# A fused attention and FFN kernel: the first FFN pieces cut into quarters that follow the pairs of heads, and a new table of due times

## The chip, the cores and the metric

The kernel runs on one core of one Trainium2 chip. The metric is the time of one execution on the device, in microseconds (us). Before the change the median of 8 runs is 224.05 us, from 223.49 to 226.14.

## What is computed

Two stages follow each other. The first is an attention in which the blocks of K and V are mixed by a matrix that five rounds of row and column normalisation make from `sort_net`. The second is an FFN with a squared ReLU on the attention's output. Cut to what matters, with B = 4 batches, H = 8 heads, S = 768 positions, D = 64, 8 blocks of 96 positions, 3072 tokens, a model width of 512 and a hidden width of 2048:

```python
P = sort_net
for _ in range(5):
    P = exp(P - max(P, -1)); P = P / sum(P, -1); P = P / sum(P, -2)
k_sorted = einsum('bhij,bhjcd->bhicd', P, k_blocks)     # and v_sorted
scores = scale * q_blocks @ k_sorted_blocks.T           # inside each block
attn   = softmax(scores) @ v_sorted_blocks
x   = attn.transpose(0, 2, 1, 3).reshape(3072, 512)
h   = maximum(x @ w_in, 0)
out = (h * h) @ w_out
```

## The kernel before

**The order.** The order of all engines is fixed when the program is built. Each step is an `Op` with an engine, an estimated cost, the steps that it depends on and, for attention steps on TensorE, a due time. `Plan.run` (L117) lays the steps out in time: TensorE takes either the head of the attention list `att` or the head of the FFN list `ffn`. An attention step goes ahead when it can begin earlier, or when its due time has come. Due times (`DUES`, L21) count FFN pieces begun (`chunks`, L150). Each list keeps its own order; the attention list is sorted by due time (L1063). The instructions are then emitted in the order of begin that the plan found, so the plan's costs (`TAIL`, L97, and the extra lateness in `SLACK`, L100) decide what stands behind what on every engine, SyncE's queue of transfers among them. None of the plan's numbers is an instruction; only the order comes out of them.

**The pairs.** Heads are worked on in four pairs per batch. A pair's 128 rows of `xT` are one of the four groups of 128 (kc) over which the FFN's first product sums. The stages of a pair are K and V (sorting by multiplication, L560, copied out of PSUM by L229 on ScalarE or L231 on VectorE), S (scores, L631, then exp on ScalarE, L654 or L663), T (transpose of V, L679), A (attention times V, L814, then a reciprocal and a product on VectorE, L824 and L825) and X (transpose into `xT`: L862 on TensorE, or a DMA transpose on SyncE, L847). In `FIRST` (L53), which orders the first half of the first batch, a capital letter gives the copy to ScalarE and a small one to VectorE.

**The batches.** The first batch is handled in two halves of 384 positions each. From the second on, K and V come in another layout. V is multiplied (V, `s_nat`, L714), copied to `vn`, written to device memory (`v_way`, L738) and read back in blocks (`vblk`, L744). K is multiplied (N, `s_nat` too), copied to `kn` and turned by a DMA transpose (Z, `kx`, L766), and q likewise (`qT`, L789). All of these transfers and the stores of results (L937) go out through SyncE, one after the other.

**The FFN.** `ffn_unit` (L880) works on half a batch, 384 tokens: 16 pieces `up`, each of four multiplications hp (L893, one per kc) into one PSUM tile of the pool `psf`, each followed by a ReLU (L901, ScalarE) and a square (L904, VectorE); then three tiles of 128 tokens, each with four pieces `down` of four multiplications op (L921). Every piece `up` depends on the `xT` of all four pairs (L883, L908). `psf` has three buffers; the first batch's K and V and the q transposes use them too, ahead of the FFN. Attention steps share two further PSUM tiles, `p2`, in turn.

**The loads.** GpSimd issues the loads of q, k, v and the weights. w_in and w_out come in four quarters each (L325 and L358). Until the FFN begins, the program fills longer waits of TensorE with multiplications by a matrix of ones (`fill`, L389); the emitting loop (L1070) decides where.

Of the kernel before, what the change touches and what calls it, by code (L numbers as in the profile page):

```python
# [8 lines left out]
FP32 = mybir.dt.float32  # L9
# [9 lines left out]


DUES = {  # L21
    (0, "K"): (-15.0, -1.0, 10, 10),
    (0, "S"): (-1.0, 11.0, 11.0, 15.0),
    (0, "T"): (-1.5, 10.0, 13.5, 19.5),
    (0, "A"): (14.0, 14.5, 18.0, 21.5),
    (0, "X"): (16.0, 23.0, 24.5, 25.0),
    (0, "W"): (1.5,),
    (1, "V"): (4.0, 20.5),
    (1, "Q"): (31.0,),
    (1, "N"): (None, 33.0),  # L30
    (1, "Z"): (None, None, 43.0, 44.0),
    (1, "S"): (33.5, 41.0, 43.0, 48.0),
    (1, "A"): (39.5, 41.5, 45.5, 52.0),
    (1, "X"): (48.0, 49.5, 49.5, 55.0),
    (2, "L"): (52.0,),
    (2, "N"): (64.0, 69.5),
    (2, "V"): (74.5, 91.5),
    (2, "Z"): (84.0, 86.0, 95.5, 96.5),
    (2, "S"): (88.5, 93.0, 97.5, 100.5),
    (2, "A"): (95.0, 99.5, 102.0, 104.0),  # L40
    (2, "X"): (96.5, 105.5, 107.5, 109.5),
    (3, "L"): (110.5,),
    (3, "N"): (120.0, 126.0),
    (3, "V"): (123.0, 141.5),
    (3, "Z"): (130.5, 138.0, 153.0, 155.5),
    (3, "S"): (143.5, 153.0, 157.5, 159.5),
    (3, "A"): (149.5, 155.0, 160.5, 162.5),
    (3, "X"): (158.5, 160.0, 161.5, 166.5),
}

FIRST = ("K0 V0 K1 v1 S0 t0 S1 k2 t1 A0 V2 S2 K3 t2 A1 V3 X0 A2 S3 t3 x1 A3 X2 x3")  # L53


class Op:


    def __init__(self, eng, cost, fn, deps, due=0, mode="full"):
        self.mode = mode  # L60
        self.engs = (eng,) if isinstance(eng, str) else eng
        self.cost = (cost,) if not isinstance(cost, tuple) else cost
        self.fn, self.deps, self.due = fn, [d for d in deps if d is not None], due
        self.begin = self.end = None


class Ring:
# [24 lines left out]
class Plan:  # L92
# [1 line left out]

    TAIL = {"PE": 0.0, "ACT": 0.09, "DVE": 0.06, "POOL": 0.0, "DMA": 0.0, "SP": 0.0, "WAY": 0.6}  # L97
    HOP = 0.06
    SWITCH = 0.1
    SLACK = {"DMA": 2.5, "WAY": 1.0}  # L100

    def __init__(self):
        self.att, self.ffn, self.rest = [], [], []
# [13 lines left out]
    def run(self):  # L117
        free = {e: 0.0 for e in self.TAIL}
        att, ffn, rest = list(self.att), list(self.ffn), list(self.rest)
        done, chunks, mode = [], 0, "full"  # L120
        self.gaps = []
        while att or ffn or rest:
            best = None
            for op in rest:
                r = self.ready(op)
                if r is None:
                    continue
                s, c, e = min(((max(r, free[e]), c, e) for e, c in zip(op.engs, op.cost)),
                              key=lambda x: x[0] + x[1])
                if best is None or s < best[0][0]:  # L130
                    best = ((s, s + c), op, e, c)
            heads = []
            for q in (att, ffn):
                if q:
                    r = self.ready(q[0])
                    if r is not None:
                        heads.append((max(r, free["PE"]), q))
                        continue
                heads.append((None, q))
            (sa, _), (sf, _) = heads  # L140
            pick = None
            if sa is not None and (sf is None or sa < sf - 0.02
                                   or (att[0].due <= chunks and sa <= sf + 0.1)):
                pick = (sa, att)
            elif sf is not None:
                pick = (sf, ffn)
            if pick and (best is None or pick[0] <= best[0][0]):
                s, q = pick
                op = q.pop(0)
                chunks += q is ffn  # L150
                e, c = "PE", op.cost[0] + self.SWITCH * (op.mode != mode)
                mode = op.mode
                op.gap = s - free["PE"]
                if s - free["PE"] > 0.01:
                    self.gaps.append((op, s - free["PE"]))
            else:
                (s, _), op, e, c = best
                rest.remove(op)
            op.begin, op.end, op.eng = s, s + c, e
            free[e] = s + c - self.TAIL[e]  # L160
            done.append(op)
        return sorted(done, key=lambda o: o.begin)
# [3 lines left out]
def kernel(  # L166
# [12 lines left out]
    B, H, S, D = q.shape  # L179
# [11 lines left out]
    KC = d_model // 128  # L191
# [6 lines left out]
    ffn = ctx.enter_context(tc.tile_pool(name="ffn", bufs=2))  # L198
    ps1 = ctx.enter_context(tc.tile_pool(name="ps1", bufs=1, space=bass.MemoryType.PSUM))
    ps2 = ctx.enter_context(tc.tile_pool(name="ps2", bufs=1, space=bass.MemoryType.PSUM))  # L200
    psf = ctx.enter_context(tc.tile_pool(name="psf", bufs=3, space=bass.MemoryType.PSUM))
# [9 lines left out]
    plan = Plan()  # L211
    rvn, rvb = Ring(2), Ring(3)
    r1, r2, rf, rh1, rh2, rob = Ring(1), Ring(2), Ring(3), Ring(3), Ring(2), Ring(3)
# [81 lines left out]
    landed = {}  # L295
# [200 lines left out]
    x_done = {}  # L496
# [201 lines left out]
    def s_nat(b, g, t, due):  # L698

        if t == 2:  # L700
            m, oldm = rvn.take()
        evs = []
        for hp in (2 * g, 2 * g + 1):
            slot, old = r2.take()
            if t == 1:
                m, oldm = rkn.take()

            def mm(e, hp=hp, slot=slot):
                src = qkv[b][t].rearrange("p (g h) x -> p g (h x)", h=HP)
                w = w_t[:, HP // 2 * b + g, :, :].rearrange("p c i -> p (c i)")  # L710
                for h in range(2):
                    r = slice(32 * (2 * (hp % 2) + h), 32 * (2 * (hp % 2) + h + 1))
                    for c in range(4):
                        nc.tensor.matmul(  # L714
                            out=p2[slot][32 * c:32 * (c + 1), h, 0:NA * D],
                            lhsT=w[r, :],
                            rhs=src[r, g, NA * D * c:NA * D * (c + 1)],
                            start=True, stop=True, tile_position=(r.start, 32 * c))

            def ev(e, hp=hp, slot=slot, m=m):  # L720
                dst = (vn_r[m][:, :, 2 * (hp % 2):2 * (hp % 2) + 2, 0:D] if t == 2
                       else kn_r[m])
                copy(e, dst, p2[slot][:, :, 0:NA * D].rearrange("p e (a d) -> p a e d", d=D))

            pe = plan.add("PE", 0.15, mm, [landed[b, t, HP * g, 0], built["t"]] + old, due,
                          mode="tile")
            readers[b].append(pe)
            op = plan.add(AD, cost_f(2 * NA * D), ev, [pe] + oldm)
            r2.use(slot, pe, op)
            evs.append(op)  # L730
            if t == 1:
                rkn.use(m, op)
                k_nat[b, hp] = m, op
        if t == 1:
            return

        def write(e):
            nc.sync.dma_start(out=v_way[b, g].rearrange("a p x -> p a x"),  # L738
                              in_=vn_r[m].rearrange("p a h x -> p a (h x)"))

        w, oldw = rvb.take()

        def read(e):
            nc.sync.dma_start(  # L744
                out=vb_r[w].rearrange("p i h x -> p (i h x)"),
                in_=v_way[b, g].rearrange("a (c i) x -> (a c) (i x)", i=NB))

        wr = plan.add("SP", 0.33, write, evs + ([loaded(b)] if b > 1 else []))
        slow = 6.0 if b == 1 else 2.0
        there = plan.add("WAY", slow, lambda e: None, [wr])  # L750
        rd = plan.add("SP", 0.33, read, [there] + oldw)
        back = plan.add("WAY", slow, lambda e: None, [rd])
        rvn.use(m, *evs, there)
        rvb.use(w, back)
        v_blk[b, g] = w, back
# [124 lines left out]
    def ffn_unit(g):  # L880
        t0 = HS * g
        b, hf = g // 2, g % 2
        xs = [x_done[b, hp, hf] for hp in range(HP)]  # L883
        t = {}
        n2, old2 = rh2.take()
        sq = []
        for nt in range(NT):
            def up(e, nt=nt):
                if nt == 0:
                    t["h2"] = ffn.tile([128, NT, HS], BF16, tag="h2", name="h2")  # L890
                t["hp", nt] = psf.tile([128, 512], FP32, tag="pf", name="hp")
                for kc in range(KC):
                    nc.tensor.matmul(  # L893
                        out=t["hp", nt][:, 0:HS],
                        lhsT=w_in_bf[:, kc, 128 * nt:128 * (nt + 1)],
                        rhs=xT[:, kc, t0:t0 + HS],
                        start=(kc == 0), stop=(kc == KC - 1))
# [6 lines left out]
                nc.vector.tensor_tensor(  # L904
                    out=t["h2"][:, nt, :], in0=t["h1", nt], in1=t["h1", nt], op=ALU.mult)

            sf, old = rf.take()
            pe = plan.add("PE", 0.65, up, xs + [landed["w_in", nt // 4]] + old, ffn=True)  # L908
            s1, old1 = rh1.take()
            r = plan.add("ACT", cost_f(HS)[0], relu, [pe] + old1)  # L910
            s = plan.add("DVE", 0.355, square, [r] + old2)
# [196 lines left out]
```

The softmax here doesn't subtract the row's maximum and nothing guards it: scores larger than these inputs give would overflow.

## Time and profile before

| What | us |
|---|---|
| median of 8 runs | 224.05 |
| the profiled execution's own time | 223.92 |
| its span | 222.1 |
| TensorE busy (fillers among it) | 213.3 |
| ScalarE busy | 120.8 |
| VectorE busy | 102.8 |
| first FFN multiplication begins | 22.19 |
| last multiplications begin (L955, 32 of them) | 214.69 |

The span runs from the first to the last event of the profile; 1.8 us of the execution's own time lie outside it. A busy time counts how long an engine had an instruction in work; neighbouring multiplications overlap, so the distance from one start to the next tells the price of one better than its length does. In a timeline each line gives start, length, engine, line, operation, output and input, and the number of neighbouring instructions that are drawn together.

The chain of waits that ended last consists of TensorE for 76% and of DMA for 16% of the span, most of the latter the loads of w_in and w_out up to 40.86 us.

### The profile page before, as it was taken

What the parts mean: (1) busy time and instruction counts of PE and PEld (TensorE: products, weight loads), DVE (VectorE), ACT (ScalarE), POOL (GpSimd) and SP (SyncE); (2) the same over time, 40 slices, a digit from 0 to 9 for tenths busy, and PEclk for the clock granted to TensorE, in tenths of its full rate; (3) what the DMA queues carried; (4) which work ended last, traced back from release to release, by engine and by line L of the source; (5) the groups of instructions that cost most, each with busy time, mean ns of one, the idle gap of its engine ahead of it and who ended that gap; (6) DMA issues with size and microseconds to landing.
All of it is one profiled execution on the core that took longest, in us unless ns stands there. A gap on an engine that the chain in (4) does not pass through costs nothing.

```text
span 222.1 us, 5101 instructions
## 1 busy us (share of the span) xinstructions
PE 213.3 (96%) x2049; PEld 119.9 (54%) x2065; DVE 102.8 (46%) x291; ACT 120.8 (54%) x249; POOL 26.5 (12%) x49
## 2 busy tenths in 40 slices
PE   8998999999999999999999999999799999999993
PEld 2576665446665555445665465446455455456562
DVE  6778476444773347502676056405655155015300
ACT  4665887217875178517863278229473276147421
POOL 7973230000000600000000330000000000000000
PEclk9999999999999999999999999999999999999999
DMA  5999999998633599189943599558982510120012
GB/s 70 200 203 207 209 206 215 209 260 231 157 75 86 96 221 221 20 227 220 199 112 84 127 182 214 119 148 188 207 173 82 118 49 3 47 94 0 3 62 80
DMA packets 46583, 31.22 MB, mean 141 GB/s; under 512 B 26016, under 2 KB 41632, under 8 KB 46560
## 3 DMA queue, kind: packets, MB, share of 16 engines
q0 software_dynamic: 12736, 13.63, 37.3%
q1 hardware_dynamic: 33824, 17.27, 31.0%
q8 instruction: 16, 0.26, 0.5%
q14 instruction: 7, 0.06, 0.1%
HBM read 29.70 MB, written 8.72 MB: 173 GB/s over the span
## 4 chain that ended last, share of the span: by engine, by line
PE 76%; DMA 16%; POOL 3%; ACT 1%; issue 1%; DVE 1%; SPq 0%; ACTq 0%
PE op L921 34%; PE hp L893 31%; DMA w_out_bf<-in_moe_w_out_dram 10%; DMA w_in_bf<-in_moe_w_in_dram 4%; PE p L631 3%; PE p L814 3%; DMA vblk<-v_way 2%; PE op L955 2%; PE p L714 2%; POOL vb L300 1%; POOL kb L300 1%; DMA p_sb<-in_sort_net_dram 1%; ACT h L901 1%; DVE h L904 0%; PE qtp L511 0%
## 5 line engine op out<-in xcount | busy, mean ns | idle before, releaser
L893 PE MATMUL hp<-xT,w_in_bf 128*128 128x384 bf16 x512 | 88.9, 326 | 0.0
L921 PE MATMUL op<-w_out_bf,h 128*128 128x512 bf16 x352 | 83.2, 379 | 1.2 <-DMA w_out_bf<-in_moe_w_out_dram 0.3
L904 DVE TENSOR_TENSOR h<-h 128x384 bf16<-128x384 bf16 x128 | 44.5, 355 | 62.8 <-ACT h L901 62.3
L901 ACT ACTIVATE h<-hp 128x384 bf16<-128x384 f32 x128 | 61.7, 495 | 19.3 <-PE hp L893 15.8
L893 PEld LDWEIGHTS <-w_in_bf 128*128 128x128 bf16 x512 | 48.1, 98 | 32.1 <-issue 1.0
L921 PEld LDWEIGHTS <-h 128*128 128x128 bf16 x368 | 34.1, 98 | 37.9 <-issue 1.3
L229 ACT COPY ob<-op 128x512 f32<-128x512 f32 (+1 forms) x24 | 13.6, 568 | 62.8 <-PE op L921 60.2
L825 DVE TENSOR_TENSOR ao<-p,rec 96x512 bf16<-96x512 f32 x32 | 22.0, 687 | 1.2
L663 ACT ACTIVATE et<-p 96x384 bf16<-96x384 f32 x48 | 19.5, 488 | 3.1 <-PE p L631 3.1
L814 PEld LDWEIGHTS <-et 96*128 96x128 bf16 x256 | 11.3, 97 | 5.8 <-issue 2.0
L824 DVE RECIPROCAL rec<-p 96x8 f32<-96x8 f32 x32 | 6.4, 200 | 16.6 <-PE p L814 16.5
L397 PE MATMUL p<-ones 128*128 128x512 bf16 (+1 forms) x36 | 10.0, 399 | 1.1 <-DVE ones L250 1.1
L1047 POOL COPY held<-xT 1x3 bf16<-1x3 bf16 (+1 forms) x2 | 0.4, 184 | 88.9 <-DMA xT<-ao 88.9
L814 PE MATMUL p<-vblk,et 96*128 96x65 bf16 x192 | 8.9, 193 | 1.3 <-DMA vblk<-v_way 1.3
L231 DVE CAST vn<-p 128x768 bf16<-128x768 f32 x6 | 5.7, 957 | 8.7 <-PE p L714 8.7
L631 PEld LDWEIGHTS <-kx 64*128 64x128 bf16 x160 | 6.1, 155 | 3.9 <-issue 3.7
L631 PE MATMUL p<-qT,kx 64*128 64x96 bf16 x160 | 7.4, 228 | 0.0
L231 DVE CAST kn<-p 128x768 bf16<-128x768 f32 x5 | 4.8, 957 | 4.8 <-PE p L714 4.8
L300 POOL DMA_DIRECT2D kb<-in_k_dram x10 | 6.4, 641 | 3.8 <-DMA w_in_bf<-in_moe_w_in_dram 2.0
L300 POOL DMA_DIRECT2D qb<-in_q_dram x8 | 6.2, 770 | 4.6 <-DMA w_out_bf<-in_moe_w_out_dram 2.0
L300 POOL DMA_DIRECT2D vb<-in_v_dram x10 | 6.3, 625 | 3.2 <-DMA w_in_bf<-in_moe_w_in_dram 2.0
L654 ACT ACTIVATE et<-p 96x768 bf16<-96x768 f32 x8 | 6.2, 803 | 0.1
(80 smaller groups left out, 112.7 us busy)
## 6 DMA issues: line engine op xcount, KB each, us to landing
out_dram<-ob SPq DMA_DIRECT2D x23, 256.0 KB, 2.2
qb<-in_q_dram POOLq DMA_DIRECT2D x8, 384.0 KB, 11.2
v_way<-vn SPq DMA_DIRECT2D x6, 396.0 KB, 4.1
vblk<-v_way SPq DMA_DIRECT2D x6, 396.0 KB, 4.1
vb<-in_v_dram POOLq DMA_DIRECT2D x6, 384.0 KB, 11.5
kb<-in_k_dram POOLq DMA_DIRECT2D x6, 384.0 KB, 10.1
w_in_bf<-in_moe_w_in_dram POOLq DMA_DIRECT2D x4, 512.0 KB, 11.8
w_out_bf<-in_moe_w_out_dram POOLq DMA_DIRECT2D x4, 512.0 KB, 19.0
```

The lines of the kernel that those rows point to most:

```text
L229: nc.scalar.copy(out=out, in_=in_)
L231: nc.vector.tensor_copy(out=out, in_=in_)
L300: nc.gpsimd.dma_start(out=dst, in_=src)
L397: nc.tensor.matmul(out=out, lhsT=ones, rhs=rhs, start=True, stop=True)
L631: nc.tensor.matmul(out=scp[:, h, BLK * n:BLK * (n + 1)], lhsT=(u.ksT[64 * h:64 * (h + 1), HS * hf + BLK * n:HS * hf + BLK * n + 128] if no ...
L663: nc.scalar.activation(out=et[:, h, 0:HS].rearrange("p (n c a) -> p n c a", c=C0, a=NA), in_=st["p"][0:96, h, 0:HS].rearrange("p (n a c) - ...
L814: nc.tensor.matmul(out=oup[:, h, 66 * n:66 * n + D + 1], lhsT=et_r[u.et[hf]][:, h, BLK * n:BLK * n + 128], rhs=(u.vs[:, NQ * hf + n, h, 0: ...
L825: nc.vector.tensor_tensor(out=u.ao[:, n0:n0 + NQ, :, :].rearrange("p n e d -> p e n d"), in0=ov[:, :, :, 0:D], in1=rec[:, :, :, None].to_b ...
L893: nc.tensor.matmul(out=t["hp", nt][:, 0:HS], lhsT=w_in_bf[:, kc, 128 * nt:128 * (nt + 1)], rhs=xT[:, kc, t0:t0 + HS], start=(kc == 0), sto ...
L901: nc.scalar.activation(out=t["h1", nt], in_=t["hp", nt][:, 0:HS], func=AF.Relu)
L904: nc.vector.tensor_tensor(out=t["h2"][:, nt, :], in0=t["h1", nt], in1=t["h1", nt], op=ALU.mult)
L921: nc.tensor.matmul(out=t["op", mt], lhsT=t["h2"][:, nt, 128 * mt:128 * (mt + 1)], rhs=w_out_bf[:, nt, :], start=(nt == 0), stop=(nt == NT ...
```

## The change

Four things are changed.

First, in the first half batch the pieces 0, 1 and 2 of the FFN's first product are no longer laid out as three steps of four multiplications. They become twelve steps of one, ordered by pair: for pair 0 one multiplication of each of the three pieces, then for pair 1, and so on. Each depends on its own pair's `xT` alone. Three PSUM tiles of `psf` are held open at once. Each step counts a quarter of a piece (`share`), so due times keep their meaning.

Second, the order of the first half of the first batch (`FIRST`) is altered: V0 comes before K0, K3 before S2, pair 3's V (T3) is copied by ScalarE and pair 0's X by VectorE, S3 goes before A2 and T3 before x1.

Third, the planner has a new class of transfer, `DRAM`, for the way of V through device memory, with a latency of 4.0 in place of 2.0 for the later batches and with a time line of its own, apart from the transposes (`WAY`).

Fourth, all due times are replaced. Together these move attention steps within the FFN's work over the whole program, and with them the order on ScalarE, VectorE and SyncE. The order on GpSimd stays as it was.

```diff
 DUES = {
-    (0, "K"): (-15.0, -1.0, 10, 10),
+    (0, "K"): (-5.0, 3.0, 11.5, 11.5),
...
-    (1, "V"): (4.0, 20.5),
-    (1, "Q"): (31.0,),
-    (1, "N"): (None, 33.0),
+    (1, "V"): (7.5, 23.0),
+    (1, "Q"): (24.0,),
+    (1, "N"): (None, 24.5),
...
-    (2, "L"): (52.0,),
-    (2, "N"): (64.0, 69.5),
-    (2, "V"): (74.5, 91.5),
-    (2, "Z"): (84.0, 86.0, 95.5, 96.5),
-    (2, "S"): (88.5, 93.0, 97.5, 100.5),
-    (2, "A"): (95.0, 99.5, 102.0, 104.0),
+    (2, "L"): (52.0,),
+    (2, "N"): (62.5, 57.0),
+    (2, "V"): (67.5, 79.0),
+    (2, "Z"): (82.0, 85.5, 87.5, 94.5),
+    (2, "S"): (90.5, 92.5, 96.0, 100.0),
+    (2, "A"): (95.5, 97.5, 100.5, 102.0),
...
-    (3, "N"): (120.0, 126.0),
-    (3, "V"): (123.0, 141.5),
-    (3, "Z"): (130.5, 138.0, 153.0, 155.5),
-    (3, "S"): (143.5, 153.0, 157.5, 159.5),
-    (3, "A"): (149.5, 155.0, 160.5, 162.5),
-    (3, "X"): (158.5, 160.0, 161.5, 166.5),
+    (3, "N"): (126.5, 139.5),
+    (3, "V"): (134.0, 144.5),
+    (3, "Z"): (136.5, 139.5, 142.0, 152.5),
+    (3, "S"): (148.5, 155.0, 157.0, 158.0),
+    (3, "A"): (154.5, 155.5, 159.0, 159.5),
+    (3, "X"): (155.5, 159.0, 160.5, 162.0),
 }
-FIRST = ("K0 V0 K1 v1 S0 t0 S1 k2 t1 A0 V2 S2 K3 t2 A1 V3 X0 A2 S3 t3 x1 A3 X2 x3")
+FIRST = ("V0 K0 K1 v1 S0 t0 S1 k2 t1 A0 V2 K3 S2 t2 A1 V3 x0 S3 A2 T3 x1 A3 X2 x3")
...
+        self.share = 1
...
-    TAIL = {"PE": 0.0, "ACT": 0.09, "DVE": 0.06, "POOL": 0.0, "DMA": 0.0, "SP": 0.0, "WAY": 0.6}
+    TAIL = {"PE": 0.0, "ACT": 0.09, "DVE": 0.06, "POOL": 0.0, "DMA": 0.0, "SP": 0.0, "WAY": 0.6, "DRAM": 3.0}
...
-    SLACK = {"DMA": 2.5, "WAY": 1.0}
+    SLACK = {"DMA": 2.5, "WAY": 1.0, "DRAM": 0.5}
...
-                chunks += q is ffn
+                chunks += op.share if q is ffn else 0
...
-        slow = 6.0 if b == 1 else 2.0
-        there = plan.add("WAY", slow, lambda e: None, [wr])
+        slow = 6.0 if b == 1 else 4.0
+        there = plan.add("DRAM", slow, lambda e: None, [wr])
         rd = plan.add("SP", 0.33, read, [there] + oldw)
-        back = plan.add("WAY", slow, lambda e: None, [rd])
+        back = plan.add("DRAM", slow, lambda e: None, [rd])
...
-        t = {}
+        t, last = {}, {}
...
-            def up(e, nt=nt):
-                if nt == 0:
+            def up(e, nt=nt, kcs=range(KC)):
+                if nt == 0 and kcs[0] == 0:
                     t["h2"] = ffn.tile([128, NT, HS], BF16, tag="h2", name="h2")
-                t["hp", nt] = psf.tile([128, 512], FP32, tag="pf", name="hp")
-                for kc in range(KC):
+                if kcs[0] == 0:
+                    t["hp", nt] = psf.tile([128, 512], FP32, tag="pf", name="hp")
+                for kc in kcs:
...
-            sf, old = rf.take()
-            pe = plan.add("PE", 0.65, up, xs + [landed["w_in", nt // 4]] + old, ffn=True)
+            if g == 0 and nt == 0:
+
+                early = [rf.take() for n in range(3)]
+                for kc in range(KC):
+                    for n in range(3):
+                        last[n] = plan.add(
+                            "PE", 0.1625, lambda e, n=n, kc=kc, up=up: up(e, n, (kc,)),
+                            [x_done[0, kc, 0], landed["w_in", 0]] + early[n][1], ffn=True)
+                        last[n].share = 1 / KC
+            if nt in last:
+                pe, sf = last[nt], early[nt][0]
+            else:
+                sf, old = rf.take()
+                pe = plan.add("PE", 0.65, up, xs + [landed["w_in", nt // 4]] + old, ffn=True)
```

More of the change, by code (lines that the diff above doesn't have):

```diff
@@ L21 @@
 DUES = {
-    (0, "K"): (-15.0, -1.0, 10, 10),
[L23 to L27, printed above, removed]
-    (1, "V"): (4.0, 20.5),
-    (1, "Q"): (31.0,),
-    (1, "N"): (None, 33.0),
[L31 to L34, printed above, removed]
-    (2, "L"): (52.0,),
-    (2, "N"): (64.0, 69.5),
-    (2, "V"): (74.5, 91.5),
-    (2, "Z"): (84.0, 86.0, 95.5, 96.5),
-    (2, "S"): (88.5, 93.0, 97.5, 100.5),
-    (2, "A"): (95.0, 99.5, 102.0, 104.0),
-    (2, "X"): (96.5, 105.5, 107.5, 109.5),
-    (3, "L"): (110.5,),
-    (3, "N"): (120.0, 126.0),
-    (3, "V"): (123.0, 141.5),
-    (3, "Z"): (130.5, 138.0, 153.0, 155.5),
-    (3, "S"): (143.5, 153.0, 157.5, 159.5),
-    (3, "A"): (149.5, 155.0, 160.5, 162.5),
-    (3, "X"): (158.5, 160.0, 161.5, 166.5),
+    (0, "K"): (-5.0, 3.0, 11.5, 11.5),
+    (0, "S"): (5.0, 11.5, 12.0, 17.0),
+    (0, "T"): (3.0, 3.0, 12.0, 16.5),
+    (0, "A"): (7.5, 14.5, 18.0, 18.5),
+    (0, "X"): (12.0, 18.0, 18.0, 22.0),
+    (0, "W"): (-4.0,),
+    (1, "V"): (7.5, 23.0),
+    (1, "Q"): (24.0,),
+    (1, "N"): (None, 24.5),
+    (1, "Z"): (None, None, 36.5, 41.5),
+    (1, "S"): (27.0, 39.5, 44.0, 50.0),
+    (1, "A"): (43.0, 44.5, 46.0, 51.0),
+    (1, "X"): (47.5, 50.0, 51.0, 54.0),
+    (2, "L"): (52.0,),
+    (2, "N"): (62.5, 57.0),
[3 more added lines that the diff above has]
+    (2, "A"): (95.5, 97.5, 100.5, 102.0),
+    (2, "X"): (98.5, 99.5, 101.5, 111.0),
+    (3, "L"): (118.0,),
+    (3, "N"): (126.5, 139.5),
[4 more added lines that the diff above has]
+    (3, "X"): (155.5, 159.0, 160.5, 162.0),
 }
-FIRST = ("K0 V0 K1 v1 S0 t0 S1 k2 t1 A0 V2 S2 K3 t2 A1 V3 X0 A2 S3 t3 x1 A3 X2 x3")
+FIRST = ("V0 K0 K1 v1 S0 t0 S1 k2 t1 A0 V2 K3 S2 t2 A1 V3 x0 S3 A2 T3 x1 A3 X2 x3")
 class Op:
```

## The prediction, made before the changed kernel was run

> **What bounds the kernel now.** I read the page's list of engines first, then the waits, then TensorE's timeline, and last SyncE's timeline and the landings of the weights.
>
> ```profile
> PE 213.3 (96%) x2049; PEld 119.9 (54%) x2065; DVE 102.8 (46%) x291; ACT 120.8 (54%) x249; POOL 26.5 (12%) x49
> PE p L814 <- DMA vblk<-v_way: 1.3, 1, 1.3
> PE op L921 <- DMA w_out_bf<-in_moe_w_out_dram: 0.3, 1, 0.3
> SPq L744 <- DMA v_way<-vn: 17.5, 3, 11.3
> ```
>
> TensorE is the bound: busy for 96% of the span, and no other engine passes 54%. So time can only come from places where it idles, waits inside a group, or runs fillers (multiplications with a matrix of ones, L397). The waits name two DMA waits of TensorE itself, 1.3 and 0.3 us.
>
> ```profile
> 18.51 0.35 PE L631 MATMUL p<-qT,kvT 64*128 64x96 bf16 x8 [0.17 <-DVE ao L825]
> 18.82 0.38 PE L679 MATMUL vbp<-ident,kvT 128*128 128x128 bf16 x4
> 19.75 0.33 PE L862 MATMUL xtp<-ident,ao 96*128 96x96 bf16 x4 [0.56 <-DVE vs L231]
> 19.92 0.42 PE L814 MATMUL p<-vs,et 96*128 96x65 bf16 x8
> 20.18 0.28 PE L397 MATMUL p<-ones 128*128 128x128 bf16 x2
> 20.53 0.33 PE L862 MATMUL xtp<-ident,ao 96*128 96x96 bf16 x4
> 20.70 0.60 PE L397 MATMUL p<-ones 128*128 128x512 bf16 x2
> 21.43 0.33 PE L862 MATMUL xtp<-ident,ao 96*128 96x96 bf16 x4
> 22.19 1.47 PE L893 MATMUL hp<-xT,w_in_bf 128*128 128x384 bf16 x8
> ...
> 40.90 1.89 PE L921 MATMUL op<-w_out_bf,h 128*128 128x512 bf16 x8 [0.33 <-DMA w_out_bf<-in_moe_w_out_dram]
> ...
> 153.28 2.77 PE L893 MATMUL hp<-xT,w_in_bf 128*128 128x384 bf16 x16
> 157.39 0.66 PE L814 MATMUL p<-vblk,et 96*128 96x65 bf16 x16 [1.34 <-DMA vblk<-v_way]
> ```
>
> Columns: start, length, engine, line, work, and in brackets the idle time before it with what ended it. The reader is to see four things. Before the first FFN work (22.19) the fillers stand from 20.18 to 20.53 and 20.70 to 21.43, 1.08 us together, because each of the last two transposes waits for its pair's softmax. At 40.90 the last quarter of w_out arrives only just. At 157.39 the fourth batch's first attention product waits for the read of vblk. Everything between is dense.
>
> ```profile
> 124.23 22.34 SPq L937 DMA_DIRECT2D out_dram<-ob  x4
> 146.71 0.38 SPq L738 DMA_DIRECT2D v_way<-vn  x1
> ...
> 152.58 0.53 SPq L744 DMA_DIRECT2D vblk<-v_way  x1
> ...
> DMA to landing us min/median/max: 16.3/19.0/21.2
> ```
>
> On SyncE the write of vn (V made on TensorE at 137.78) stands behind four stores until 146.71, the read back goes out at 152.58, and lands 4.76 us later in the chain of waits. The last line is from the view of w_out_bf: the fourth load, issued at 19.68, lands at 19.68 + 21.2 = 40.9.
>
> **What the Trainium skill says.** "TensorE: Matmul & The Clock Gate", section "Wait — 56ns, not 53.3ns?": warm matmuls start N/2.4 GHz plus some 2.5 ns apart, 162.5 ns for 384 columns. The trace agrees: the 64 hp of 176.63 to 187.03 take 162.5 ns each. So the order in which those of three pieces are taken is free. "PSUM — Partial Sum Buffer", "The four PSUM rules": opening a sum clears the flags of its own bank only, so three open sums in three banks cost nothing extra; no run here shows it yet. "DMA: Bandwidth & Descriptors", "Queues, rings and completion order": an engine alternates between its queues packet by packet. This agrees: the first v_way write, beside the weight loads, took 11.7 us, in quiet stretches 3.4 to 4.3.
>
> **Part 1, the first three FFN pieces (12 of the 64 hp of the first half batch).** Before, none starts until the last pair's xT is copied. After, the order is one hp, transpose of pair 2, four hp, transpose of pair 3, sort of pair 0, one hp, wtp, six hp, and both late filler groups are gone. The added multiplications are none, the total stays 64. FIRST also moves V0 before K0, S2 behind K3, and copies pair 3's V by ScalarE. Followed step by step with the durations of the trace (S 0.28, vbp 0.31, AV 0.26 to 0.35, exp 0.75, norm 0.2 + 0.69): S0 slips 0.28 because K0 is copied second and a filler pair comes in; A0 and A1 slip 0.22; A3 lands near 20.1, before 19.92; x3 still near 21.5, because the chain of pair 3 (AV, 0.9 of VectorE) sets it. So the first stage doesn't get shorter, but 5 hp of 0.163 run in its gaps. At 23.5 us before has the sort of pair 0 and 8 hp behind it, after the sort, 12 hp and wtp: 4 x 0.163 + 0.16 = 0.81 ahead, less about 0.1 for lone groups: 0.7.
>
> What is late next: w_out. The last quarter is first needed (before at 40.57, waited for until 40.90) after one AV (0.25) and two xtp (2 x 0.17) more than before: 0.6 us of work moved ahead of it. Arrival is then 40.57 - 0.7 + 0.6 = 40.5, and it waits until 40.9 again. Since the GpSimd queue that issues these loads is unchanged instruction for instruction, I let them land at 40.9. The gain carried past that point is the moved work, **0.6** (0.3 if Part 1 gives nothing, 0.9 if the load lands earlier too). The hp of pieces 3 to 15 need w_in quarters that land at 22 to 27 us, well before.
>
> **Part 2, V of the fourth batch.** The DRAM class of the planner prices write and read at 4.0 apart from the transposes, and the dues move. From the start of the fifth half batch's hp (126.87 before): A0 came after hp64, op48, hp36; after it comes after hp64, op48, hp56, 20 x 0.163 = 3.3 us later. V0 itself is 5.2 us later (24 op first), but its write stood behind the store of the second tile anyway; on SyncE it goes out at +19.0, then kx 1.27, qT 1.24, kx, store 0.5, qT, then the read at +25.2, landing at +29.2 to +30.0. A0 is reached at +31.8. The stall of **1.34** goes, with 1.8 us to spare. The second read goes out at +32.4 and lands by +37.2; needed at +40.4.
>
> **Part 3, the third batch.** Before, K and V products (L714, 0.31 each) were spread over 83 to 106 us. After, four stand in one op phase with only four op (0.87) between. Each fills both PSUM slots, which take 0.80 (ScalarE) and 0.96 (VectorE) to empty: the pair at 90.80 and 92.08 shows the cost, 1.82 us for 1.49 of work, 0.33. In the block I take 0.25 + 0.15 + 0.15 = 0.55: **+0.2** net (0 to +0.7). SyncE then has, ahead of vblk's read, from about 95.3: write 0.4, kx, store, write, qT, kx, qT, store, together 6.8, and 0.9 more because a transpose right behind a v_way write took 1.55 to 1.70 before: issue near 103.0, landing after 3.1 to 6.3 (median 4.1): 106.1 to 109.3. A0 of that batch is reached near 108.2. I take no stall, and keep up to 3.4 for a rival.
>
> **Part 4, small waits for PSUM slots.** Scores at 65.65, 69.73 and 111.34 last 0.87, 0.90 and 0.83 against 0.63 undisturbed: 0.24 + 0.27 + 0.20 = 0.7, which stand too close behind an AV; in the new order they have eight op, or a half group, between. **-0.7**. New close ones (AV straight behind a score, scores of the last pair four hp behind an AV): **+0.3** (0 to +0.9). At the start of the seventh half batch the last transpose stands behind a store: out near +45.2, landing +48.1 (2.9), needed by the fourth hp at +48.0: **+0.1**. V of the second batch's second half moves about 2.5 us later, behind two stores; its read lands near 61, needed past 66: nothing.
>
> Sum: -0.6 - 1.34 + 0.2 - 0.7 + 0.3 + 0.1 = -2.04. On the profiled execution's own 223.92 (span 222.1 and 1.8 around it) that is 221.9; this execution lies 0.13 below the median shown, so 222.0.
>
> **Rivals.**
> - *Only the vblk stall goes.* If the loads of w_out slip with TensorE, or new slot waits eat Parts 1 and 4: 223.92 - 1.34 + 0.2 = 222.8. For it: w_out's wait is already there. Against: the moved AV and transposes do not need w_out.
> - *The stall moves.* A0 of the third batch waits some 1.7 for vblk: 223.92 - 2.04 + 1.7 = 223.6. For it: my estimates have 108.2 needed and 106.1 to 109.3 landing, hardly any spare.
> - *Slower: SyncE becomes the bound in the third batch.* Ahead of the read stand two kx and two qT; single ones have taken up to 1.70 (kx) and 2.68 (qT) instead of 1.27 and 1.24. All four at that length are 3.7 more than 6.8, so issue at 106 and landing at 110 to 112, a stall of up to 3.4: 223.92 - 2.04 + 3.4 = 225.3. It begins to cost when the read goes out past 104.1 (108.2 less 4.1), and decides against the change past some 106.2, 2.1 later. Against: the medians are the short values, and the one qT of 2.68 stands behind a read, not ahead of it.
> - *It doesn't do what it says* (the interleaving is lost): excluded by the built order given above.
>
> **How the numbers follow.** Chances: forecast 0.56, only the stall 0.15, moved stall 0.11, slower 0.18. The forecast alone reaches from 220.9 (Part 1 at 0.9, no new slot waits, a few tenths more) to 223.0 (Parts 3 and 4 at their dear ends). The whole range takes in the second, the third and part of the fourth: 220.9 to 224.9, leaving out about 1 in 10 on each side. Half a per cent, 1.12 us, is about what a measurement can tell: below 222.93 counts as faster: 0.53 of the forecast and 0.09 of the first rival, 0.62. Within: 0.03 + 0.06 + 0.10 + 0.01 = 0.20. Slower: 0.18.
>
> **What would show it.** Right: hp beside xtp near 20.5 with no filler after 14.2; the op at 40.9 still waiting, some tenths; no wait of PE on vblk; the later op phases without scores over 0.7. Wrong: an AV near 108 waiting for vblk; a first hp that begins past 21; L714 groups of over 0.6 in the block near 92; w_out landing past 41.2.

## The result and the profile after

The changed kernel takes 227.49 us (median of 11 runs, 226.0 to 228.94) where the kernel before took 223.92 on the same chip (32 runs, 223.49 to 226.58). The ratio is 1.0144, with a 95% interval from 1.0118 to 1.017. It is slower, by 3.6 us; the prediction was 222.0 with a range of 220.9 to 224.9. The profiled execution took 227.75 us, its span is 225.9. Of the executions on record, four kept the full clock and took 226.0 to 226.3 us, and the others had a mean clock of 0.985 to 0.992 and took 227.0 to 228.9.

The page of the changed kernel, its list of engines and the granted clock in forty slices:

```profile
PE 215.2 (95%) x2046; PEld 120.3 (53%) x2063; DVE 104.7 (46%) x291; ACT 122.0 (54%) x249; POOL 26.5 (12%) x49
...
PEclk9999999999999999999969999999999999999999
```

TensorE has nearly the same number of instructions as before and is busy 1.9 us longer, in a span 3.8 us longer. One slice, the 21st (from 113 to 118.6 us), shows a lowered clock. The view of waits has one long wait of TensorE that before did not have, while the two waits shown there before, for vblk and for w_out, are gone:

```profile
PE p L633 <- DMA qT<-qi: 3.1, 1, 3.1
```

Where it lies is best seen from stage to stage. The table gives the start of the first FFN multiplication (hp) of each half batch, and the steps between them, in us from the start of the span:

| | first hp | 1 to 2 | 2 to 3 | 3 to 4 | 4 to 5 | 5 to 6 | 6 to 7 | 7 to 8 | 8 to end |
|---|---|---|---|---|---|---|---|---|---|
| before | 22.19 | 27.82 | 28.16 | 22.23 | 26.47 | 22.02 | 27.74 | 20.76 | 24.7 |
| after | 20.49 | 28.97 | 28.21 | 23.01 | 30.97 | 22.02 | 26.67 | 20.88 | 24.7 |
| difference | -1.70 | +1.15 | +0.05 | +0.78 | **+4.50** | 0 | -1.07 | +0.12 | 0 |

The front gains 0.55 (the first two columns together), the fourth batch's attention gains 1.07, and the third batch's attention, which runs inside the half batches 3 and 4, loses 5.28. That one stage is the whole loss. TensorE's timeline of the changed kernel shows the three places (columns as in the prediction; hp is now L896, op L936, scores L633, the attention products L816, the V and K products L716):

```profile
20.07 0.33 PE L864 MATMUL xtp<-ident,ao 96*128 96x96 bf16 x4 [0.67 <-ACT vs L231]
20.24 0.42 PE L816 MATMUL p<-vs,et 96*128 96x65 bf16 x8
20.49 0.33 PE L896 MATMUL hp<-xT,w_in_bf 128*128 128x384 bf16 x1
20.85 0.33 PE L864 MATMUL xtp<-ident,ao 96*128 96x96 bf16 x4
21.01 0.82 PE L896 MATMUL hp<-xT,w_in_bf 128*128 128x384 bf16 x4
21.74 0.34 PE L864 MATMUL xtp<-ident,ao 96*128 96x96 bf16 x4
...
41.10 2.75 PE L936 MATMUL op<-w_out_bf,h 128*128 128x512 bf16 x11
...
94.34 0.65 PE L716 MATMUL p<-vb,w_t 32*32 32x384 bf16 x16
...
109.31 0.66 PE L816 MATMUL p<-vblk,et 96*128 96x65 bf16 x16
109.81 1.46 PE L896 MATMUL hp<-xT,w_in_bf 128*128 128x384 bf16 x8
114.37 0.46 PE L633 MATMUL p<-qT,kx 64*128 64x96 bf16 x8 [3.10 <-DMA qT<-qi]
114.76 1.46 PE L896 MATMUL hp<-xT,w_in_bf 128*128 128x384 bf16 x4
...
163.92 0.66 PE L816 MATMUL p<-vblk,et 96*128 96x65 bf16 x16
```

The hp stand where the fillers stood (20.49 and 21.01), the work at 41.10 no longer waits for w_out, and the fourth batch's first attention product (163.92) no longer waits for vblk. In the third batch the first attention product (109.31) does not wait either. But the scores of pair 2, at 114.37, wait 3.10 us for their q. The four hp after them last 1.46 us where four last 0.81 or 0.82 elsewhere.

SyncE's own timeline of the changed kernel shows what stood ahead of that q:

```profile
103.83 0.54 SPq L952 DMA_DIRECT2D out_dram<-ob  x1
104.42 0.60 SPq L746 DMA_DIRECT2D vblk<-v_way  x1
105.11 1.21 SPq L768 DMA_TRANSPOSE kx<-kn  x1
106.41 0.54 SPq L746 DMA_DIRECT2D vblk<-v_way  x1
107.00 2.71 SPq L791 DMA_TRANSPOSE qT<-qi  x2
109.80 3.71 SPq L768 DMA_TRANSPOSE kx<-kn  x1
```

Both reads of vblk go out within 2 us of each other, with one transpose of K between them, and the q transposes of pairs 2 and 3 (107.00, drawn together) come right behind the second read. In the kernel before, the last q transpose went out at 105.8, 6.7 us ahead of the second read (112.47). From the view of qT between 95 and 115 us, the time from issue to landing, after:

```profile
DMA to landing us min/median/max: 3.4/5.4/7.2
```

and from the same view before, 90 to 115 us:

```profile
DMA to landing us min/median/max: 2.6/3.1/4.2
```

The 7.2 is pair 2: the chain that ended last has that transfer from 107.00 for 7.24 us, to 114.24. The view of vblk puts the second read's landing 7.3 us after its issue, at 113.7, so the transpose landed just behind the read that went out before it.

The wait has a second part. For 1.6 us of the time in which TensorE waits, almost nothing moves on any DMA queue, and the read and the transposes behind it land only after that. The view of stretches shows it (columns: the stretch and its length, PE, PEld, DVE, ACT and POOL busy, then the granted clock, the DMA share and GB/s):

```profile
111.70:113.30 1.60, 0.00 (x0) 0.00 (x0) 0.62 (x3) 0.00 (x0) 0.00 (x0) 1.00 0.04 4
```

Such a halt, of 1.0 to 1.7 us and at 3 to 18 GB/s, stands between 108.8 and 113.4 us in seven of the experiments below as well. In these runs the order on SyncE decides whether the q of pair 2 has landed before it.

### The profile page after: what moved, and what is told of

Same layout as the page of the kernel before. It is cut to its first block, busy times and chain, and to the rows that moved or that the text cites. A ratio compares the mean times of both kernels' runs of the same rounds, so it can differ in the third digit from the quotient of the medians.

```text
span 225.9 us, 5082 instructions
## 1 busy us (share of the span) xinstructions
PE 215.2 (95%) x2046; PEld 120.3 (53%) x2063; DVE 104.7 (46%) x291; ACT 122.0 (54%) x249; POOL 26.5 (12%) x49
## 4 chain that ended last, share of the span: by engine, by line
PE 86%; DVE 4%; DMA 3%; ACT 2%; issue 2%; POOL 1%; SPq 0%; POOLq 0%; ACTq 0%; DVEq 0%
PE hp L896 35%; PE op L936 35%; PE p L633 4%; PE p L816 4%; DMA qT<-qi 3%; PE p L716 2%; PE op L970 2%; PE vbp L681 1%; PE xtp L864 1%; PE p L598 1%; PE tp L562 1%; DVE p_sb L379 1%; ACT h L904 1%; DVE ao L827 1%; POOL qb L302 1%
## 5 line engine op out<-in xcount | busy, mean ns | idle before, releaser
L896 PE MATMUL hp<-xT,w_in_bf 128*128 128x384 bf16 x512 | 90.2, 329 | 0.0
L936 PE MATMUL op<-w_out_bf,h 128*128 128x512 bf16 x351 | 84.1, 379 | 1.1 <-issue 0.3
L896 PEld LDWEIGHTS <-w_in_bf 128*128 128x128 bf16 x512 | 48.5, 98 | 32.5 <-issue 1.6
L936 PEld LDWEIGHTS <-h 128*128 128x128 bf16 x368 | 33.7, 98 | 37.1 <-issue 1.2
L816 PEld LDWEIGHTS <-et 96*128 96x128 bf16 x256 | 11.5, 98 | 4.8 <-issue 0.4
L633 PE MATMUL p<-qT,kx 64*128 64x96 bf16 x160 | 7.8, 231 | 3.1 <-DMA qT<-qi 3.1
L633 PEld LDWEIGHTS <-kx 64*128 64x128 bf16 x160 | 6.3, 155 | 7.5 <-issue 7.4
L399 PE MATMUL p<-ones 128*128 128x512 bf16 (+1 forms) x34 | 9.0, 390 | 1.1 <-DVE ones L252 1.1
L816 PE MATMUL p<-vblk,et 96*128 96x65 bf16 x192 | 9.4, 195 | 0.0
L231 ACT CAST vn<-p 128x768 bf16<-128x768 f32 x6 | 4.8, 800 | 5.2 <-PE p L716 5.2
```

What stands on the lines that cost most here:

```text
L231: nc.scalar.copy(out=out, in_=in_)
L399: nc.tensor.matmul(out=out, lhsT=ones, rhs=rhs, start=True, stop=True)
L633: nc.tensor.matmul(out=scp[:, h, BLK * n:BLK * (n + 1)], lhsT=(u.ksT[64 * h:64 * (h + 1), HS * hf + BLK * n:HS * hf + BLK * n + 128] if no ...
L816: nc.tensor.matmul(out=oup[:, h, 66 * n:66 * n + D + 1], lhsT=et_r[u.et[hf]][:, h, BLK * n:BLK * n + 128], rhs=(u.vs[:, NQ * hf + n, h, 0: ...
L896: nc.tensor.matmul(out=t["hp", nt][:, 0:HS], lhsT=w_in_bf[:, kc, 128 * nt:128 * (nt + 1)], rhs=xT[:, kc, t0:t0 + HS], start=(kc == 0), sto ...
L936: nc.tensor.matmul(out=t["op", mt], lhsT=t["h2"][:, nt, 128 * mt:128 * (mt + 1)], rhs=w_out_bf[:, nt, :], start=(nt == 0), stop=(nt == NT ...
```

## The experiments

The main theory (A) was this: the loss is the order on SyncE in the third batch, the q transpose behind the second vblk read, and the slower clock after that wait. The rivals put it into TensorE's own order there (the block of V and K products, waits for PSUM slots), into the front, or into the fourth batch. Twelve runs, all against the kernel before on the same chip:

| run | us | ratio to before | 95% interval | 3 to 4 | 4 to 5 | 6 to 7 |
|---|---|---|---|---|---|---|
| the change | 227.49 | 1.0144 | 1.0118 to 1.017 | 23.01 | 30.97 | 26.67 |
| second read behind | 224.29 | 0.9978 | 0.9959 to 0.9998 | 23.02 | 27.37 | 26.67 |
| kept warm | 226.45 | 1.007 | 1.0044 to 1.0096 | 23.01 | 29.48 | 26.67 |
| V later | 223.7 | 0.9959 | 0.9939 to 0.9979 | 22.44 | 27.88 | 26.67 |
| front alone | 224.46 | 0.9993 | 0.9955 to 1.003 | 22.24 | 26.47 | 28.42 |
| q early | 223.39 | 0.9942 | 0.9919 to 0.9965 | 23.02 | 26.46 | 26.67 |
| q early, N spread | 222.72 | 0.9894 | 0.9844 to 0.9944 | 22.43 | 26.47 | 26.68 |
| third batch back | 222.76 | 0.9895 | 0.9857 to 0.9932 | – | – | – |
| third batch back, again | 222.65 | 0.9917 | 0.9895 to 0.9939 | 22.23 | 27.04 | 26.67 |
| old FIRST | 222.54 | 0.9914 | 0.989 to 0.9939 | 22.43 | 26.47 | 26.67 |
| whole pieces | 224.07 | 0.9979 | 0.9961 to 0.9998 | 22.43 | 26.47 | 26.67 |
| fourth batch alone | 223.23 | 0.9895 | 0.9844 to 0.9947 | 22.23 | 26.46 | 26.88 |
| third batch alone | 228.63 | 1.0142 | 1.0107 to 1.0177 | 22.80 | 26.46 | 31.56 |

The last three columns are the stages of the table above. No stage is read from the first "third batch back", whose profiled execution took 358.5 us.

**The second read behind the transposes.** From the changed kernel, only the planner's price of the third batch's second write is raised:

```diff
-        there = plan.add("DRAM", slow, lambda e: None, [wr])
+        there = plan.add("DRAM", slow + (4.0 if (b, g) == (2, 1) else 0.0), lambda e: None, [wr])
```

TensorE's order stays as it is; on SyncE the second read moves from before the two q transposes to behind them and the next K transpose.

> Only the order on SyncE differs from the changed kernel: the third batch's second vblk read goes out three transfers later, behind qT, qT and kx. Theory A (the transposes' data queue behind that read's data): qT of pair 2 lands within 4 us of its issue near 106.4, the 3.10 us wait at the scores goes, the clock behind it stays at 1.0, and the time falls from 227.5 by 3.1 plus 1.5 to 2 of slow clock: 222.4 to 223.0. Theory B (SyncE simply has too many transposes to issue here, whatever their order): the wait shrinks by one issue, 0.6 us, at most, and the time stays above 226.5. If the read itself becomes late for pair 2's attention product (needed near 116), a new wait of up to 1 us appears there and the time is up to 224.

SyncE's timeline, and then TensorE's, of this kernel:

```profile
104.54 0.53 SPq L746 DMA_DIRECT2D vblk<-v_way  x1
105.16 1.22 SPq L768 DMA_TRANSPOSE kx<-kn  x1
106.43 2.66 SPq L791 DMA_TRANSPOSE qT<-qi  x2
109.18 2.37 SPq L768 DMA_TRANSPOSE kx<-kn  x1
111.61 0.57 SPq L746 DMA_DIRECT2D vblk<-v_way  x1
```

```profile
112.11 0.46 PE L633 MATMUL p<-qT,kx 64*128 64x96 bf16 x8 [0.85 <-DVE h L907]
112.49 0.82 PE L896 MATMUL hp<-xT,w_in_bf 128*128 128x384 bf16 x4
```

The wait falls from 3.10 to 0.85 us, and the hp after it are at full speed. The stage from 4 to 5 falls from 30.97 to 27.37, and the median by 3.2 us, to 224.29; the 222.4 to 223.0 that was expected is missed, since 0.85 of wait and the block of products are left. The bracket names a square of VectorE, but those scores do not use it; the q transpose of pair 2, issued at 106.43, landed at 111.93, 5.5 us later. It is still behind the first read and the K transpose, and the halt of the queues (3 GB/s from 109.4 to 111.1) falls into its way. So one read moved on one queue, with nothing changed on TensorE, gives back most of the loss.

**Kept warm.** Fillers stand before the waiting scores, 14 multiplications by the matrix of ones whose results nothing uses. They are added work and let no transfer go sooner:

```diff
+                if (u.b, u.hp, hf) == (2, 2, 0):
+                    fill(4.7, slot)
```

> The changed kernel with 14 filler multiplications (3.0 us) on TensorE just ahead of the scores that wait. The wait itself can't get shorter. If TensorE's clock drops because it idles 3.5 us (windows show 0.70 for 114.4 to 120): the work behind the scores runs at full clock, hp x4 takes 0.65 and not 1.40, and the time falls by 1.5 to 2: 225.5 to 226.0. If the slowness behind the wait comes from PSUM slots and ScalarE's backlog instead, the time stays at 227.0 to 227.5.

TensorE's timeline of this kernel:

```profile
111.09 3.19 PE L399 MATMUL p<-ones 128*128 128x512 bf16 x14
114.21 0.46 PE L635 MATMUL p<-qT,kx 64*128 64x96 bf16 x8
114.59 0.82 PE L898 MATMUL hp<-xT,w_in_bf 128*128 128x384 bf16 x4
```

and the busy times from 114.4 to 120 us, first of the changed kernel, then of this one (columns as above):

```profile
114.40:120.00 5.60, 5.55 (x60) 3.29 (x60) 2.43 (x7) 3.61 (x9) 0.00 (x0) 0.70 0.33 65
```

```profile
114.40:120.00 5.60, 5.50 (x73) 3.46 (x73) 2.85 (x8) 4.78 (x12) 0.00 (x0) 1.00 0.15 27
```

The scores begin at nearly the same time, but the clock stays at 1.00 where it had a mean of 0.70. From their start to the next half batch the changed kernel takes 131.65 - 114.37 = 17.28 us and this one 130.14 - 114.21 = 15.93. The slow clock alone costs the difference, 1.35 us, in the profiled executions. The other 3.15 of the 4.50 is the wait. The median falls by 1.04 us, to 226.45, above the 225.5 to 226.0 that was expected. In this execution q was there earlier: the transpose of pair 2, issued at 106.89, landed 6.1 us later, at 113.0, and the queues slowed but did not halt (42 GB/s from 111.4 to 112.1). The fillers, and not q, held the scores until 114.21; without them the wait would have been some 1.9 us (an estimate: 113.0 less 111.09).

**V later.** From the changed kernel, the due time of the second V product of the third batch is set back to that of before.

```diff
-    (2, "V"): (67.5, 79.0),
+    (2, "V"): (67.5, 91.5),
```

> The changed kernel with one due time put back: the third batch's second V (79.0 to 91.5). It moves that V out of the block of four K and V products on TensorE and its write and read behind the transposes of pairs 2 and 3. Theory A: the 3.10 us wait and the slow clock go, and 0.2 to 0.4 of the block too: 222.0 to 222.8. Theory B (too many transposes at once): four qT and four kx still stand in the same stretch, the wait stays at 2 to 3 us, and the time above 226.

The wait for q is gone, since the second read now goes out at 115.27, behind all q transposes. In its place comes a wait of 0.36 us for vblk at 119.06. The stage from 4 to 5 takes 27.88, 1.42 more than with q early below: 0.36 is that wait, 0.31 is the work of the V product, which again stands in this stage, and the rest is waits for PSUM slots around it (its second eight multiplications, at 106.54, take 0.45 where the first eight take 0.28). The stage from 3 to 4 is shorter because the V product has left it. The time is 223.7, above the 222.0 to 222.8 that was expected: a second way of parting read and transpose, with the same effect on the wait.

**The front alone.** The kernel before with the quarter steps and the new `FIRST` alone, and with the old dues.

> The kernel before with the first three FFN pieces by quarters and the new FIRST alone; due times and transfer classes as before. By the prediction's first part: up to 0.6 us faster, 223.3. Rival: the new FIRST delays the last pairs by what the quarters save, and w_out's landing swallows the rest: 223.7 to 224.0. Neither explains any of the 3.5 us loss.

Nothing is gained (0.9993; 224.46, where 223.3 or 223.7 to 224.0 was expected). The first hp begins at 20.49, as in the changed kernel, but the three open sums end together and the next hp waits for the ReLU of the first:

```profile
24.74 1.15 PE L895 MATMUL hp<-xT,w_in_bf 128*128 128x384 bf16 x6
26.35 4.06 PE L895 MATMUL hp<-xT,w_in_bf 128*128 128x384 bf16 x24 [0.46 <-ACT h L903]
```

A further 0.39 us goes to a wait for vb at 43.10, so that the second half batch starts at 50.34 (before 50.01, after 49.46). The wait for vblk in the fourth batch grows from 1.3 to 2.0 us, as the stage from 6 to 7 shows (28.42 against 27.74).

**q early.** On top of the read moved behind, the q transposes of the third batch's first two pairs are put ahead of its first v_way write. SyncE had stood idle there in the changed kernel, from 92.7 to 96.08 us.

```diff
+    order = plan.run()
+    early_q = [q_sps[2, 0], q_sps[2, 1]]
+    order = [op for op in order if op not in early_q]
+    at = order.index(writes[2, 0])
+    order[at:at] = early_q
```

> As e2_read_behind, and besides the q transposes of pairs 0 and 1 of the third batch go out on SyncE ahead of the first v_way write, where SyncE stood idle for 3.4 us waiting for vn. Nothing else moves. Theory A (the 0.85 us still waited for at pair 2's scores is its q transpose, which stood behind the first vblk read's data and landed 5.5 us after its issue): it goes out 2.5 to 3 us earlier, lands by 109.5, the wait goes, and the time falls by 0.8 to 1.0 against e2_read_behind: 223.2 to 223.6 where the kernel before has 224.3. Rival (the wait is VectorE's norm of the AV before, as the chain of waits of that run names VectorE): scores still begin 0.8 late, 224.0 to 224.4.

SyncE's timeline of this kernel, and TensorE's:

```profile
93.03 3.49 SPq L792 DMA_TRANSPOSE qT<-qi  x2
96.62 0.53 SPq L741 DMA_DIRECT2D v_way<-vn  x1
...
102.47 0.38 SPq L747 DMA_DIRECT2D vblk<-v_way  x1
102.94 1.29 SPq L769 DMA_TRANSPOSE kx<-kn  x1
104.28 2.70 SPq L792 DMA_TRANSPOSE qT<-qi  x2
```

```profile
111.46 0.45 PE L633 MATMUL p<-qT,kx 64*128 64x96 bf16 x8
```

The transpose of pair 2, issued at 104.28, lands 4.7 us later, before the queues slow down (75 GB/s from 110 to 111). The rest of the wait is gone, and the stage from 4 to 5 takes 26.46, as before the change. What remains is the stage from 3 to 4, 23.02 against 22.23.

**q early, and the K products spread.** The same, with one more row of due times put back:

```diff
-    (2, "N"): (62.5, 57.0),
+    (2, "N"): (64.0, 69.5),
```

> As e5_q_early, and the third batch's two K products (N) get the due times of the kernel before (64.0, 69.5), so that the first stands in hp work again and the block of four has three. If the block costs what its starts show (0.66 us over the work itself, 0.25 of it before op x4): 0.3 to 0.5 less than e5_q_early: 222.8 to 223.2. If only the number of products per PSUM slot counts, wherever they stand: the same as e5_q_early within 0.2.

The stage from 3 to 4 falls from 23.02 to 22.43: the block of four V and K products cost 0.59 of the 0.78. 222.72 us.

**The third batch put back.** From the changed kernel, all due times of the third batch but its loads are those of before. It was run twice.

> The changed kernel with all the third batch's due times of the kernel before (21 numbers); front, second batch, fourth batch and transfer class stay changed. If the whole loss lies in the third batch's due times: its stretch (third and fourth half batch... of the FFN, from 78 to 127 us) takes 48.7 to 49.2 again and not 54, while 0.35 before it and 1.07 behind it stay gained: 222.8 to 223.3 where the kernel before has 224.3. If part of the loss comes from the transfer class or from the earlier batches' shift: 224 or more.

> e6_third_batch_back once more, for an undisturbed profile: 222.8 at the median of the pair; the stretch from the start of hp of the third half batch to that of the fifth takes 48.7 to 49.2 as in the kernel before, with q of pair 2 landing ahead of its scores.

222.76 and 222.65 us: front and fourth batch keep their gains, and the loss is gone with the third batch's due times.

**The old FIRST, and whole pieces.** Both from the version with q early and N spread: one takes back `FIRST` and keeps the quarters, the other takes back the quarters (`if False:` for `if g == 0 and nt == 0:`) and keeps `FIRST`.

> As e7_q_early_n_spread (222.72), with FIRST of the kernel before; the quarters stay. If the new FIRST is what delays the first stage (S0 at 14.19 instead of 13.96, x1 at 20.07 instead of 19.75): x1 comes 0.3 earlier again, and 0.1 to 0.4 of it pass the landing of w_out at 40.9: 222.3 to 222.6. If the two orders are worth the same: within 0.2 of 222.7.

> As e7_q_early_n_spread, with the first three FFN pieces whole again (fillers return in the gaps before the first hp). The prediction's first part says the quarters are worth 0.6 us past w_out's landing: 223.3. What e4_front_alone showed says some 0: the same as e7_q_early_n_spread within 0.3, with the wait for w_out shorter by what the front loses.

`FIRST` is worth nothing that can be told: 222.54 with the old one, 222.72 with the new. The quarters are worth 1.35 us with these due times (224.07 less 222.72, on two chips), where 0.6 or nothing was expected. With whole pieces the fillers are back and the FFN begins late:

```profile
20.70 0.28 PE L399 MATMUL p<-ones 128*128 128x128 bf16 x2
...
21.22 0.60 PE L399 MATMUL p<-ones 128*128 128x512 bf16 x2
...
22.72 0.82 PE L897 MATMUL hp<-xT,w_in_bf 128*128 128x384 bf16 x4
```

First hp 22.72 against 20.48, second half batch 50.94 against 49.55, which is 1.39. The same quarters, with the new `FIRST`, were worth nothing under the old due times.

**The fourth batch alone, the third batch alone.** From the kernel before, each with the planner's DRAM class and the new due times of one batch.

> The kernel before with the new transfer class and the fourth batch's new due times alone. The prediction's second part: the 1.34 us wait for vblk goes, less the new waits for PSUM slots: from start of hp of the fifth half batch to that of the seventh 48.7 and not 49.8, the time 0.9 to 1.3 below before: ratio 0.994 to 0.996. If the wait's end is taken up by SyncE elsewhere: ratio 0.998 to 1.002.

> The kernel before with the new transfer class and the third batch's new due times alone (and the load step's, which must follow it). TensorE's order in that batch is that of the changed kernel from the block of K and V products on, nearly to the letter, but on SyncE the planner puts pair 2's q transpose ahead of the second vblk read instead of behind it. Theory A (the place behind the read costs the time): no wait of 3 us, at most 0.9 as in e2_read_behind, and the block's 0.4: 0.4 to 1.6 above before, ratio 1.002 to 1.007. If TensorE's order itself is what costs (the scores simply come too early for any transpose): the 3.1 us wait and the slow clock come back, ratio 1.02.

The fourth batch alone removes the wait for vblk; the stage from 6 to 7 is 0.86 shorter, and the span 221.5 against 222.1. On that chip the kernel before has a median of 225.09, where it had 223.92 on the first one, so the stages say more than the ratio. The third batch alone did not do what was expected of the total: 228.63 us. But its third batch is nearly whole. With the old orders around it the q transpose of pair 2 (105.74) comes ahead of the second read (107.13), the scores do not wait, and the two stages take 22.80 + 26.46 = 49.26 against 48.70. The same due times thus cost 0.56 us of TensorE's own time when the queue's order is good. What it lost lies in the fourth batch, as TensorE's timeline shows, and below it SyncE's:

```profile
160.29 1.04 PE L814 MATMUL p<-vblk,et 96*128 96x65 bf16 x16 [3.18 <-DMA vblk<-v_way]
```

```profile
153.32 2.57 SPq L789 DMA_TRANSPOSE qT<-qi  x1
155.99 0.53 SPq L744 DMA_DIRECT2D vblk<-v_way  x1
```

Under the old due times the DRAM class puts one more q transpose ahead of the fourth batch's first read. It goes out at 155.99 instead of 152.58, and the wait grows from 1.34 to 3.18. A further 0.35 goes to a wait for q at 152.40, and from 160.29 to 166 us the clock has a mean of 0.71. It is again one place on SyncE's queue, and again the clock after it.

**The best version.** The versions at 222.5 to 222.8 us (third batch back; q early with N spread, with either `FIRST`) are faster than both kernels, by 0.8 to 1.1% against the one before on the same chips. These chips gave the kernel before medians of 224.40 and 224.75; against the 223.92 of the first chip it would be 0.5 to 0.6%.

## Why the prediction was wrong

**Part 1 (-0.6): right in size, partly by luck.** The first hp came at 20.49 (predicted near 20.5), the fillers after 14.2 us are gone, and the second half batch begins 0.55 us sooner. I had said that the work at 40.9 would still wait for w_out; it does not. The fourth load, issued at 19.60, landed 21.0 us later at 40.6, and with the moved work ahead of it TensorE came to it at 41.10. The 0.55 is also no gain of the quarters by themselves. With them under the old due times the second half batch begins 0.33 later than before (front alone, 50.34), and with the new due times and whole pieces 0.93 later (50.94); only both together give 49.46 to 49.55. The prediction had one term where the runs show two that depend on each other.

**Part 2 (-1.34): right in mechanism.** A0 of the fourth batch does not wait. The stage gained 1.07. The missing 0.27 fits new waits for PSUM slots, of scores (165.82, 170.30) and of attention products (168.56, 175.77), 0.1 to 0.2 each, of which the stage had two before; Part 4 had 0.3 for them.

**Part 3 (+0.2, no stall): here the prediction failed.** The step is the sentence "I take no stall". It followed SyncE's queue as far as the first read, and there it was nearly right: the read went out at 104.42 (I had 103.0), landed at 108.5, and A0 at 109.31 did not wait. It never asked what stands behind the *second* read, which the new due times bring within 2 us of the first. There stands the q transpose of pair 2, for which the prediction has no term. It landed 7.24 us after its issue, behind the second read and after the halt of the queues, and TensorE stood for 3.10. The block of products was mis-sized too: 0.59 of it is shown by spreading N, and the half batch lost 0.78 in all, where I took 0.2 with 0.7 as the dear end.

**A term that was missing: the clock.** No step priced what TensorE's rate does after a long wait. It cost 1.35 us, over two fifths of the wait. The Trainium skill, "TensorE: Matmul & The Clock Gate", section "What's actually happening", says that the array's clock falls to half after an idle window of some 3.4 us, and rises again after as long a busy one. The trace agrees on the fall to half and on its length, 3.4 us:

```profile
114.80:118.20 3.40, 3.40 (x25) 1.77 (x25) 1.23 (x3) 2.49 (x6) 0.00 (x0) 0.50 0.39 73
```

At 118.52 four hp take 0.81 again. The wait before it was shorter than the page's window: 3.10 us were enough here, and 3.18 in the third batch alone, while after 1.34 (before, from 157.39) and 2.0 us (front alone) the clock stayed at 1.00.

**Part 4 (-0.7 and +0.3): half right.** The scores at 65.65 and 69.73 did lose their waits, but the second batch gained nothing (28.21 against 28.16 from 2 to 3): the waits moved to other places, such as an attention product at 67.43. Slot waits change place when the order changes; I counted those that went in full and those that come in part.

**The sum.** -0.55 + 0.05 + 0.78 + 4.50 - 1.07 + 0.12 = +3.83 on a span that grew by 3.8. My sum of -2.04 had the front and the fourth batch within 0.3 each and missed the third by 5.1.

**The rivals.** The slower one, SyncE as the bound in the third batch, had the right engine and the right stage. Its wait (3.4) is near the measured one by chance, since its transfer was the wrong one, and its 225.3 lacked clock and block: 3.10 + 1.35 + 0.78 against 3.4. It was given 0.18. "Only the stall goes" and "the stall moves" did not happen in the way described. What was excluded, that the interleaving is lost, was rightly so.

**What stays open.** How the 7.24 us divide is known only in part. In the kept-warm run, with the same order on SyncE and no full halt, the transpose took 6.1, so some 1.1 of it can be put down to the halt (an estimate, 7.24 less 6.1, from one execution of each). Shared bandwidth is no reason for the halt, with 4 GB/s moving. A load of instructions, 16 KB on a queue of its own, stands in the trace from 111.65 to 112.61, and one stands beside the halt with the second read behind (108.82 to 110.47) and with V later (109.08 to 110.45) too; whether it causes the halt no run tests. No run used another queue than SyncE's for the q transposes either.

## What to carry to other kernels

When due times move, follow the queue of transfers past the first one that is needed: write down every transfer that stands behind each large read, and who waits for it, because a small transpose behind a read of 396 KB landed here just after the read. A wait of some 3 us on TensorE is priced with the slower multiplications after it, here over two fifths as much again. And a part that gains nothing alone can be worth something with the rest of a change: undo parts from the finished version as well as adding them to the old one.

## What the runs showed of the hardware

The transfers issued on SyncE landed in the order of their issue, all 69 of them in each of five traces (before, the change, second read behind, q early, third batch alone), and a q transpose, which took 2.6 to 4.2 us before, took 7.2 behind two reads and a halt. The Trainium skill, "DMA: Bandwidth & Descriptors", section "Queues, rings and completion order", says that each DMA engine takes up its descriptors in the order of their ring, but also that completion is not first in, first out for one issuing engine; these traces show no case of the latter. Most transposes hold SyncE for 1.21 to 1.31 us (23 of 31 in the changed kernel), but the one issued at 109.80 held it for 3.71, until 113.51, just past the halt. And keeping TensorE busy with idle multiplications through a wait of 3 us was worth 1.35 us of clock.
